# A recurrence and two MLPs in one kernel: input loads from GpSimd's queue, raw weight bits loaded two steps ahead, six result buffers, the triangular inverse begun later, products masked by VectorE

## The chip, the core and the metric

The kernel runs on one core of a Trainium2 chip, in one launch. A core has TensorE (PE) for matrix products, VectorE (DVE), ScalarE (ACT) and GpSimd (POOL) for elementwise work, and SyncE (SP), which in this kernel only issues DMA transfers. Each engine has one program and works through it in order; semaphores tie the engines together. A queue that issues transfers is such a program too: a transfer that waits holds up all that stands behind it on the same engine. The metric is device time in microseconds of one execution.

## The reference

The inputs are six arrays of 4 batches, 8 heads, 768 steps and 40 channels, and the weights of two MLPs. The recurrence goes over the 768 steps; `x` then passes through both MLPs (3072 tokens, 320 channels, 2048 hidden).

```python
for t in range(S):
    y[:, :, t] = np.einsum('bhd,bhde->bhe', rt, state)
    Sa = np.einsum('bhde,bhe->bhd', state, at)
    state_decay = state * wt[:, :, None, :] - np.einsum('bhd,bhe->bhde', Sa, bt)
    state = state_decay + np.einsum('bhd,bhe->bhde', vt, kt)
...
h = x @ w_in;  g = np.maximum(h, 0.0) ** 2;              x = g @ w_out
h = x @ w_in;  g = h * np.clip(h + 3.0, 0.0, 6.0) / 6.0; x = g @ w_out
```

All weights come as 64-bit floating point numbers and are turned into 32-bit ones on the core.

## The kernel before

**The recurrence.** The 768 steps are cut into 12 chunks of 64 steps, times 4 batches: 48 units, `i` = 0 to 47, four to a chunk. A unit is brought in by `load_pre` (its decays, keys and so on, one tile `IN` of 104 x 1029 numbers; two `IN` tiles take turns) and `load_main` (tiles `VS` and `VR`). `pre_steps` makes scaled rows: running products of the decays forwards (`EE`, L550) and backwards (`RV`, L569) by VectorE, then the scaled `RK` (L562) and `KBt` (L577) by GpSimd. `f1a` multiplies `KBt` by `RK` on TensorE (L586), copies one half of the product to `TB` and every second unit stores it to DRAM (`DT<-TB`, L592). `f1b` copies the other half to `RK` by ScalarE (L600) and multiplies it by a triangular mask on GpSimd (L601).

**The inverse.** Once the four units of a chunk have been through `f1`, `inv_gen` inverts the triangular matrices of the chunk by substitution. It loads them back from DRAM (`ML<-DT`, four loads, L622), does 31 rounds of two VectorE instructions (L632, L635), stores the result (`DIT`, `DI`) and loads it back in two shapes (`TB<-DIT` L645, `AI<-DI` L647). `merge_p` (L656) and `merge_x` (L667) put two half-size inverses together before unit 4c of the chunk is solved. `inv_gen` is a generator that runs ahead of the units: `begin` runs its loads as soon as the chunk is complete, then waits for three slots and six more ticks, and from there each `tick` adds one VectorE instruction. `need_inv` makes sure that it is done in time.

**The order of the work.** Each turn of the main loop issues the stages of neighbouring units in the order of `ORDER` (`ORDER0` before the first MLP has input): `rhs`, `umm`, `f1`, `kt`, `gmm`, `st`, `vumm`, `ys`, `mp`, `mx`, and four slots `M`. A slot takes one piece of the first MLP (or a few idle products, L817), then gives five ticks to the inverse and runs one step of the weights' conversion. `pre` runs `pre_steps` for a unit some nine ahead, with a tick after each of five steps, and then `load_pre` for the unit after next. In `ys` VectorE makes `SY` (L722), the output `XT` (L724) and the new state `STK` (L727), which `st` (L741) transposes.

**The MLPs.** A group is 512 tokens; each MLP has 6 groups. A piece is either `project_in` (8 matmuls, L222 to L226, then the activation by ScalarE and VectorE) or `out1`/`out2` (8 matmuls, L249 to L253, or 12, L261 to L263) for one of 16 slices of the hidden layer. The products are done with weights and activations each split into a high and a low part. `store1`/`store2` copy a finished group from PSUM and store it; `store2` copies four tiles `os` (L837) into a pool of three buffers and stores each (L840).

**The conversion.** `convert` turns 32 tiles of 64-bit weights to 32-bit: load of the raw `bits` (L83), then shifts and masks by VectorE (L97, L99), ScalarE (L96, L104) and GpSimd (L105), a product by VectorE (L109), a rounded copy (L122) and the rest (L154). One call of the generator is one step, in which six stages of six neighbouring tiles are issued, the load first. For the first MLP it runs from the slots, early in the recurrence, and stores the low parts (L139). For the second it runs beside the last pieces of the first, one step after every piece (`self.steps = 1`); it also stores every converted tile to DRAM (`W<-res`, L117), for `general_path`, a branch for inputs with extreme decays, whose instructions do not appear in the trace.

## Time and profile before

| what | value |
|---|---|
| median of 3 runs | 1394.53 us (1392.88 to 1398.54) |
| the profiled execution's own time | 1400.85 us |
| its span, first to last instruction | 1399.1 us |
| busy: PE, DVE, ACT, POOL | 1182.9, 841.3, 609.9, 390.7 us |
| mean granted TensorE clock | 0.899 |

Times in the trace are counted from the first instruction. A group of instructions is named by its line, engine and tiles, written out<-in. "Idle before" is the idle time of the engine just ahead of an instruction, and the name behind the arrow is what ended it. SPq is SyncE's queue of transfers.

### The profile page before, as it was taken

To read this page: it belongs to the slowest core of one execution; us is meant where nothing else is said; L and a number is where in the kernel's file an instruction comes from. 1 tells how busy PE (TensorE), PEld (TensorE's weight loads), DVE (VectorE), ACT (ScalarE), POOL (GpSimd) and SP (SyncE) were. 2 spreads that over 40 slices of the span, in tenths; PEclk is the share of its full clock that TensorE was granted. 3 is DMA by queue.
4 is the path that set the end of the run, shared out by engine and by line. 5 is a ranking of instruction groups with operands and counts; after the bars stand their busy time and mean duration, and the time that the engine had idled before them with its cause. 6 is when DMAs were issued, how large, how long until landed. Compare 5 with 4: busy or idle time off the path is not lost.

```text
span 1399.1 us, 25891 instructions
## 1 busy us (share of the span) xinstructions
PE 1182.9 (85%) x9682; PEld 1008.2 (72%) x9682; DVE 841.3 (60%) x1857; ACT 609.9 (44%) x1456; POOL 390.7 (28%) x564
## 2 busy tenths in 40 slices
PE   3178677798989999998989999876898989898895
PEld 3167567687777777777777788655697979797884
DVE  7847796767494948576765642599843434344332
ACT  4245554444544445454544443466533434333331
POOL 5685535333424433333433000255300000000000
PEclk9657767799999999999999999988999999999998
DMA  5546656565657465655654552587601010010000
GB/s 126 102 103 184 136 149 156 145 143 118 131 140 146 113 154 142 141 117 141 143 124 98 123 129 75 168 264 228 183 1 49 1 49 24 26 31 19 7 13 22
DMA packets 257221, 152.73 MB, mean 109 GB/s; under 512 B 201792, under 2 KB 220864, under 8 KB 257088
## 3 DMA queue, kind: packets, MB, share of 16 engines
q1 hardware_dynamic: 243264, 113.24, 34.2%
q10 hardware_dynamic: 13824, 37.75, 9.0%
q8 instruction: 79, 1.29, 0.4%
q14 instruction: 54, 0.44, 0.1%
HBM read 115.30 MB, written 35.65 MB: 108 GB/s over the span
## 4 chain that ended last, share of the span: by engine, by line
PE 48%; DMA 19%; DVE 17%; SPq 4%; issue 4%; ACT 4%; POOL 3%; DVEq 0%; ACTq 0%; POOLq 0%
PE h L222 9%; DMA DT<-TB 5%; PE h L224 4%; PE o L261 4%; PE o L262 4%; PE o L263 4%; DVE INV L635 3%; DVE TMP L632 3%; DMA out_dram<-os 3%; DMA W<-res 2%; PE h L225 2%; PE h L226 2%; SPq L622 2%; PE o L249 2%; PE a L586 2%
## 5 line engine op out<-in xcount | busy, mean ns | idle before, releaser
L240 DVE TENSOR_TENSOR gs<-g,gs 128x512 fp32r<-128x512 f32 x192 | 149.9, 781 | 77.8 <-ACT gs L234 65.9
L632 DVE TENSOR_TENSOR TMP<-ML,INV 128x126 f32<-128x126 f32 (+22 forms) x341 | 107.5, 315 | 77.2 <-DMA ML<-DT 69.6
L601 POOL TENSOR_TENSOR RK<-RK,mask 64x256 f32<-64x256 f32 x96 | 78.3, 816 | 254.0 <-ACT RK L600 238.1
L232 DVE SCALAR_TENSOR_TENSOR g<-r,h 128x512 f32<-128x512 f32 x96 | 66.0, 687 | 133.9 <-ACT r L231 133.9
L261 PE MATMUL o<-w_out,gs 128*128 128x320 f32 x384 | 121.0, 315 | 22.1 <-DVE os L837 20.6
L105 POOL TENSOR_TENSOR bits<-res,bits 128x384 int32<-128x384 int32 (+1 forms) x64 | 70.3, 1100 | 223.6 <-DMA wl<-LI 124.5
L231 ACT ACTIVATE r<-h,cst 128x512 f32<-128x512 f32 x96 | 66.2, 689 | 137.5 <-PE h L226 135.8
L262 PE MATMUL o<-w_lout,gs 128*128 128x320 f32 x384 | 120.1, 313 | 0.0
L263 PE MATMUL o<-w_out,gs 128*128 128x320 f32 x384 | 120.0, 312 | 0.0
L237 DVE TENSOR_TENSOR g<-r 128x512 f32<-128x512 f32 x96 | 66.5, 692 | 81.5 <-ACT r L236 81.5
L635 DVE TENSOR_TENSOR INV<-INV,TMP 128x126 f32<-128x126 f32 (+22 forms) x341 | 109.8, 322 | 8.3
L234 ACT CAST gs<-g 128x512 fp32r<-128x512 f32 x96 | 59.5, 620 | 97.4 <-DVE g L232 97.4
L222 PE MATMUL h<-xm,wl 128*128 128x512 f32 x192 | 78.5, 409 | 25.4 <-DMA wl<-LI 25.4
L261 PEld LDWEIGHTS o<-w_out,gs 128*128 128x128 f32 x384 | 73.7, 192 | 28.0 <-DVE os L837 21.9
L249 PE MATMUL o<-gs,wo_hi 128*128 128x512 f32 x192 | 90.6, 472 | 2.5 <-DVE os L827 1.7
L236 ACT ACTIVATE r<-h 128x512 f32<-128x512 f32 x96 | 57.0, 593 | 68.5 <-PE h L226 64.7
L562 POOL TENSOR_TENSOR RK<-IN,EE 40x256 f32<-40x256 f32 x82 | 66.4, 810 | 69.2 <-DVE EE L550 66.1
L687 ACT ACTIVATE VR<-a 40x256 f32<-40x256 f32 x96 | 36.3, 378 | 112.7 <-PE a L685 112.1
L222 PE MATMUL h<-xm,wi_hi 128*128 128x512 f32 x192 | 83.8, 437 | 1.9 <-ACT xm L208 1.9
L250 PE MATMUL o<-gs,wo_hi 128*128 128x512 f32 x192 | 82.7, 431 | 2.0 <-DVE gs L240 2.0
L251 PE MATMUL o<-gs,wl 128*128 128x512 f32 x192 | 81.9, 427 | 0.7 <-DMA wl<-LO 0.7
L577 POOL TENSOR_TENSOR KBt<-IN,RV 104x256 f32<-104x256 f32 x78 | 72.4, 948 | 32.5 <-DVE TMP L632 11.8
(159 smaller groups left out, 2953.1 us busy)
## 6 DMA issues: line engine op xcount, KB each, us to landing
wl<-LI ACTq DMA_DIRECT2D x48, 384.0 KB
wl<-LO ACTq DMA_DIRECT2D x48, 384.0 KB
IN<-in_pre_dram SPq DMA_DIRECT2D x44, 418.0 KB
bits<-in_moe_w_in_dram SPq DMA_DIRECT2D x32, 384.0 KB
bits<-in_moe_w_out_dram SPq DMA_DIRECT2D x32, 320.0 KB
VR<-in_vr_dram SPq DMA_DIRECT2D x96, 80.0 KB
DT<-TB SPq DMA_DIRECT2D x24, 256.0 KB
xr<-X SPq DMA_DIRECT2D x12, 512.0 KB
```

The lines of the kernel that those rows point to most:

```text
L222: nc.tensor.matmul(h, w[p][:, k], xm[:, k], start=(k + p == 0), stop=False)
L240: nc.vector.tensor_tensor(out=gs[:, 1], in0=g, in1=gs[:, 0].bitcast(FP32), op=ALU.subtract)
L249: nc.tensor.matmul(acc[d], hi, gs[:, 0], start=a, stop=False)
L250: nc.tensor.matmul(acc[d], hi, gs[:, 1], start=False, stop=False)
L251: nc.tensor.matmul(acc[d], lo, gs[:, 0], start=False, stop=z)
L261: nc.tensor.matmul(acc[q], gs[:, 0, s], hi, start=a, stop=False)
L262: nc.tensor.matmul(acc[q], gs[:, 0, s], lo, start=False, stop=False)
L263: nc.tensor.matmul(acc[q], gs[:, 1, s], hi, start=False, stop=z)
L577: e.tensor_tensor(out=kb_of(i)[:, :, 64 * x:64 * x + 64], in0=kb[:, :, x, :], in1=rr, op=ALU.mult)
L601: nc.gpsimd.tensor_tensor(out=o, in0=o, in1=mask[P].unsqueeze(1).to_broadcast([64, NP, 64]), op=ALU.mult)
L632: eng.tensor_tensor(out=tmp, in0=ml[:, s, s + 1:32].unsqueeze(2).to_broadcast([128, n, w]), in1=inv[:, s, 0:w].unsqueeze(1).to_broadcast([ ...
L635: eng.tensor_tensor(out=inv[:, s + 1:32, 0:w], in0=inv[:, s + 1:32, 0:w], in1=tmp, op=ALU.subtract)
```

## The change

It makes these edits:

- `load_pre` issues the load of `IN` from GpSimd's queue instead of SyncE's, from unit 11 on.
- `convert` issues the load of raw bits for two steps ahead, at the end of a step, instead of for one ahead at its start. Tile counts and buffers are the same.
- `f1b` multiplies the product by the mask in one VectorE instruction for each half, straight from PSUM; ScalarE's copy and GpSimd's product are gone.
- `begin` waits for five slots and no further ticks. In `ys` `STK` is made ahead of `XT`, and the three ticks come after all three.
- `piece` runs the second conversion after two of three pieces.
- `store2` takes two of its four tiles from the pool `m_o2` (two buffers) and two from the tags `wi` and `wo` of the pool `m_rot` (two buffers each), which the first MLP used for low weights.
- The stores `W<-res` are gone; `general_path` converts the raw bits itself where it needs them.

```diff
         def fourth(k):
             f, part = order[k]
             v, hi = res[k].bitcast(FP32), high_of(k)
-            if w["second"]:
-                nc.sync.dma_start(out=w["full"][f][:, 384 * part:384 * part + n_of[part]], in_=v)
-            else:
+            if not w["second"]:
                 rest[k] = scratch("rest", k).bitcast(F32R)
...
         n = len(order)
         load(0)
+        load(1)
         yield
         for r in range(n + 5):
-            if r + 1 < n:
-                load(r + 1)
             for lag, stage in ((5, sixth), (4, fifth), (3, fourth), (2, third), (1, second), (0, first)):
                 if 0 <= r - lag < n:
                     stage(r - lag)
+            if r + 2 < n:
+                load(r + 2)
             yield
...
-        for _ in range(self.steps):
+        if self.steps and (self.n_in + self.n_out) % 3:
             next(self.aside, None)
...
-        nc.sync.dma_start(out=in_of(i), in_=pre_in[c, b])
+        (nc.gpsimd if i > lag + 2 else nc.sync).dma_start(out=in_of(i), in_=pre_in[c, b])
...
         for h in range(2):
             P = slice(64 - 64 * h, 128 - 64 * h)
-            o = rk[P, :, 64 * h:64 * h + 64]
-            nc.scalar.copy(out=o, in_=ps[P, :, 64 * h:64 * h + 64])
-            nc.gpsimd.tensor_tensor(out=o, in0=o, in1=mask[P].unsqueeze(1).to_broadcast([64, NP, 64]), op=ALU.mult)
+            s = slice(64 * h, 64 * h + 64)
+            nc.vector.tensor_tensor(out=rk[P, :, s], in0=ps[P, :, s],
+                                    in1=mask[P].unsqueeze(1).to_broadcast([64, NP, 64]), op=ALU.mult)
...
             nc.vector.tensor_tensor(out=sy, in0=ps[:, :, 64:104], in1=stk, op=ALU.add)
-            tick()
+            nc.vector.tensor_tensor(out=stk, in0=sy, in1=E[:, :, 64:65].to_broadcast([104, NP, 40]), op=ALU.mult)
         nc.vector.tensor_tensor(out=x[:, :, b % 2, :], in0=ps[:, :, 0:64], in1=E[:, :, 0:64], op=ALU.mult)
-        tick()
-        if i + NB < NS:
-            nc.vector.tensor_tensor(out=stk, in0=sy, in1=E[:, :, 64:65].to_broadcast([104, NP, 40]), op=ALU.mult)
-            tick()
+        tick(3)
...
-    skip = [0]
-
     def begin():
-        skip[0] = 6 if moe.plan else 0
         next(gens[0][0])
-        gens[0][1] = 3 if moe.plan else 0
+        gens[0][1] = 5 if moe.plan else 0
...
             if not gens or gens[0][1]:
-                return
-            if skip[0]:
-                skip[0] -= 1
                 return
...
             for q in range(4):
-                o = opool.tile([128, DM], FP32, name="os")
+                o = (opool if q < 2 else moe.rot).tile([128, DM], FP32, tag=("os", "os", "wi", "wo")[q], name="os")
...
-        opool = hctx.enter_context(tc.tile_pool(name="m_o2", bufs=3))
+        opool = hctx.enter_context(tc.tile_pool(name="m_o2", bufs=2))
```

TensorE's program is the same instructions in the same order before and after. On the other engines the order moves, at three places above all.

SyncE's queue early in the recurrence, while the first MLP's weights are converted, around the last store of chunk 2's rows (`DT`): before.

```order
L592 DMA DT_164<-TB_131 2x64x512
L83 DMA bits<-in_moe_w_out_dram 128x640
L139 DMA LI_201<-rest 128x384
L532 DMA IN_98<-in_pre_dram 104x1029
L622 DMA ML<-DT_164 32x32x32 x4
L83 DMA bits<-in_moe_w_out_dram 128x640
L139 DMA LI_201<-rest 128x384
```

The same place of the same queue in the changed program.

```order
L605 DMA DT_164<-TB_131 2x64x512
L137 DMA LI_201<-rest 128x384
L83 DMA bits<-in_moe_w_out_dram 128x640
L635 DMA ML<-DT_164 32x32x32 x4
L137 DMA LI_201<-rest 128x384
L83 DMA bits<-in_moe_w_in_dram 128x768
```

The load of `IN` no longer stands ahead of the inverse's loads and the bits; it stands on GpSimd right behind the product `KBt` that frees the tile. The bits that follow are those of one tile later.

VectorE at the start of the inverse of chunk 4, once the first MLP runs in the slots: before.

```order
L696 TENSOR_TENSOR GV_138<-a,mask 128x8x64
L237 TENSOR_TENSOR g<-r 128x512
L240 TENSOR_TENSOR gs<-g,gs 128x512
L632 TENSOR_TENSOR TMP<-ML,INV 128x31
L635 TENSOR_TENSOR INV<-INV,TMP 128x31
L632 TENSOR_TENSOR TMP<-ML,INV 128x30
L635 TENSOR_TENSOR INV<-INV,TMP 128x30
L722 TENSOR_TENSOR SY_147<-a,STK_146 104x160
```

The same stretch of VectorE's program in the changed kernel, up to the first instruction of the inverse.

```order
L735 TENSOR_TENSOR SY_147<-a,STK_146 104x160
L736 TENSOR_TENSOR STK_146<-SY_147,EE_120 104x160
L737 TENSOR_TENSOR XT_148<-a,EE_120 104x4x64
L613 TENSOR_TENSOR RK_100<-a,mask 64x4x64 x2
L563 SCALAR_TENSOR_TENSOR EE_120<-IN_99,d_97 104x260
L567 TENSOR_SCALAR EC_163<-EE_120 104x4
L577 RECIPROCAL EC_163<-EC_163 104x4
L579 SCALAR_TENSOR_TENSOR DR_152<-flags,EC_163 104x4
L582 SCALAR_TENSOR_TENSOR RV_151<-IN_99,DR_152 104x260
L236 TENSOR_TENSOR g<-r 128x512
L239 TENSOR_TENSOR gs<-g,gs 128x512
L645 TENSOR_TENSOR TMP<-ML,INV 128x31
```

The first wait for `ML` now stands behind `ys` of the next unit, the two masked products, that unit's row scaling and one more piece. All later instructions of the inverse, its stores and its loads back move by one slot too (by two in chunk 3).

VectorE in the conversion of the second MLP's weights, between two activations of the first MLP (`g`, `gs`): before.

```order
L237 TENSOR_TENSOR g<-r 128x512
L240 TENSOR_TENSOR gs<-g,gs 128x512
L109 SCALAR_TENSOR_TENSOR res<-bits 128x320
L97 TENSOR_SCALAR res<-bits 128x384
L99 SCALAR_TENSOR_TENSOR res<-bits,res 128x384
L154 TENSOR_TENSOR w_lout<-res,w_out 128x320
L109 SCALAR_TENSOR_TENSOR res<-bits 128x384
L97 TENSOR_SCALAR res<-bits 128x320
L99 SCALAR_TENSOR_TENSOR res<-bits,res 128x320
L237 TENSOR_TENSOR g<-r 128x512
```

The same part of VectorE's program in the changed kernel.

```order
L236 TENSOR_TENSOR g<-r 128x512
L239 TENSOR_TENSOR gs<-g,gs 128x512
L109 SCALAR_TENSOR_TENSOR res<-bits 128x320
L97 TENSOR_SCALAR res<-bits 128x384
L99 SCALAR_TENSOR_TENSOR res<-bits,res 128x384
L236 TENSOR_TENSOR g<-r 128x512
```

Between two activations stand now one or two steps of the conversion, before always two. The whole conversion lies beside 26 pairs of `g` and `gs` in the changed program, the last 9 of them of the second MLP, against 18 before, of which one.

## Rows read from the trace of the kernel before

**Rows 1.** Busy time of each engine in four stretches (us, instructions), clock, DMA.
```profile
90.00:262.00 172.00, 125.98 (x1226) 113.24 (x1226) 128.92 (x286) 84.30 (x243) 86.29 (x111) 0.70 0.62 155
278.00:805.00 527.00, 484.99 (x5005) 399.46 (x5006) 356.75 (x934) 252.85 (x681) 183.99 (x278) 0.95 0.58 132
895.00:1005.00 110.00, 80.81 (x284) 61.79 (x285) 101.95 (x154) 67.32 (x138) 57.79 (x48) 0.84 0.69 219
1015.00:1065.00 50.00, 50.00 (x280) 45.29 (x280) 21.42 (x33) 19.91 (x31) 0.00 (x0) 1.00 0.08 22
```

**Rows 2.** Waits of TensorE, 1010 to 1400 us: total, times, longest.
```profile
PE o L261 <- DVE os L837: 20.6, 5, 4.2
```

**Rows 3.** The chain that ended last, second MLP: start us, us, what.
```profile
1066.34 5.92 DMA out_dram<-os
...
1322.90 5.79 DMA out_dram<-os
...
1381.02 5.83 DMA out_dram<-os
```

**Rows 4.** Timeline of TensorE at the first group's end, idle time in brackets.
```profile
1072.92 0.63 PE L261 MATMUL o<-w_out,gs 128*128 128x320 f32 x1 [4.19 <-DVE os L837]
```

**Rows 5.** Lines on VectorE by shape, 895 to 1000 us: busy, mean ns, idle before.
```profile
L97 DVE TENSOR_SCALAR res<-bits 128x384 uint32<-128x384 uint32 x16 | 8.7, 543 | 1.8 <-DMA W<-res 1.0 <-POOL bits L105 0.8
```

**Rows 6.** Waits of VectorE, 278 to 805 us.
```profile
DVE TMP L632 <- DMA ML<-DT: 68.1, 8, 9.8
```

**Rows 7.** Waits of TensorE, 278 to 805 us.
```profile
PE a L741 <- DVE TMP L632: 25.1, 8, 4.3
```

**Rows 8.** The chain that ended last, transfers of two inverses.
```profile
305.01 9.73 DMA DT<-TB
...
316.32 4.06 DMA ML<-DT
...
820.81 2.14 DMA AI<-DI
```

**Rows 9.** Timeline of SyncE's queue, second load of AI for chunk 4.
```profile
361.24 0.48 SPq L647 DMA_DIRECT2D AI<-DI  x1
```

**Rows 10.** Timeline of TensorE, first merge of chunks 4 and 11.
```profile
369.09 0.59 PE L656 MATMUL a<-AI,TB 32*64 32x32 f32 x14
...
822.46 0.30 PE L656 MATMUL a<-AI,TB 32*64 32x32 f32 x2
```

**Rows 11.** Lines on VectorE by shape, 278 to 805 us.
```profile
L724 DVE TENSOR_TENSOR XT<-a,EE 104x256 f32<-104x256 f32 x32 | 13.3, 416 | 0.0
```

**Rows 12.** Timeline of GpSimd within an inverse: start us, us, group.
```profile
401.37 1.52 POOL L601 TENSOR_TENSOR RK<-RK,mask 64x256 f32<-64x256 f32 x2 [8.18 <-ACT RK L600]
```

**Rows 13.** Timeline of VectorE at the same time.
```profile
401.09 0.29 DVE L632 TENSOR_TENSOR TMP<-ML,INV 128x126 f32<-128x126 f32 x1
401.42 0.84 DVE L635 TENSOR_TENSOR INV<-INV,TMP 128x126 f32<-128x126 f32 x1
402.29 0.76 DVE L632 TENSOR_TENSOR TMP<-ML,INV 128x136 f32<-128x136 f32 x1
```

**Rows 14.** Waits of VectorE, 90 to 262 us.
```profile
DVE res L97 <- DMA bits<-in_moe_w_out_dram: 35.3, 9, 6.9
```

**Rows 15.** Waits of SyncE's queue, 90 to 262 us.
```profile
SPq L532 <- DVE RV L569: 24.3, 5, 8.7
SPq L532 <- POOL KBt L577: 20.6, 7, 12.3
```

**Rows 16.** The chain that ended last, the first loads of IN.
```profile
1.70 6.06 DMA IN<-in_pre_dram
...
18.50 8.57 DMA in_e<-in_pre_dram
```

**Rows 17.** Timelines: issue of a load of IN (SyncE), its first reader (VectorE).
```profile
280.36 0.35 SPq L532 DMA_DIRECT2D IN<-in_pre_dram  x1
...
299.39 0.70 DVE L550 TENSOR_TENSOR_SCAN EE<-IN,d 104x260 f32<-104x260 f32 x1
```

21 lines of the change are left out of this document (17 added, 4 removed).

## The prediction

> **What bounds the kernel now.** I looked first at the busy time by stage, since the limits differ. In the second MLP (1015 to 1065 us) TensorE is busy all the time at full clock; in 278 to 805 us it is busy 485.0 of 527; in the two conversion stages VectorE is the fuller engine, 128.9 of 172 early and 102.0 of 110 late [rows 1]. So I asked in each stage what interrupts the engine that sets its pace, with the views of waits, and then took the price from the timeline or the chain.
>
> At the end of each group of the second MLP TensorE waits for VectorE's copy of a result, 4.19 us the first time and 20.6 in five [rows 2, 4], and that copy waits for a store of `os` to land, 5.8 to 5.9 us [rows 3]: four tiles go into three buffers. In the recurrence VectorE stands idle for 68.1 us in eight waits for `ML` [rows 6]; `SY` and `STK` are queued behind the waiting instruction, `st` waits for them, and TensorE loses 25.1 us there [rows 7]. Early, VectorE waits 35.3 us for raw bits [rows 14], while SyncE's queue stands 24.3 + 20.6 us at the load of `IN` [rows 15], with the bits behind it.
>
> **The change part by part.**
>
> *Result buffers.* From the first wait to the fifth, four groups take 1322.90 - 1066.34 = 256.6 us, 64.1 each [rows 3]. Undisturbed, 280 matmuls take 50.00 us [rows 1]; a slice has 8 + 12 matmuls, a group 16 slices, so 320 matmuls or 57.1 us. A boundary costs 7.0 us: the 4.2 of waiting and a restart at the low clock. With four free buffers the copies wait for nothing, TensorE has the next `project_in` to do meanwhile, and five boundaries give 35. At the end the fourth copy no longer waits 5.83 us for the first store [rows 3]; less an estimated 1.4 for its own time and the three stores issued ahead of its own, 4.4. Sum 39.4; if a boundary keeps a microsecond, 34.
>
> *Second conversion.* Here VectorE is busy 93% and TensorE 73% [rows 1], so the stores `W<-res` cost little: the wait for them on VectorE is 1.0 us [rows 5]. What helps is the pace. Before, 110 us carry 18 pairs of activations beside the conversion, and the 8 pairs that follow run at TensorE's pace, 8 x 3.57 = 28.6; together 138.6. After, all 26 pairs lie beside it: VectorE has 102.0 us of work and eight slices of the second MLP more, at 21.42 / 14 = 1.53 each [rows 1]: 114.2, at the same 93% 123.2. Gain 15.4. With VectorE full it would be 24.4. If the longer overlap with GpSimd stretches more of VectorE's work, I put the floor at 8.
>
> *Later inverse.* The eight stalls cost 25.1 us [rows 7] plus the slow clock behind them: a mean granted clock of 0.95 over 527 us [rows 1] is 53 us at the lower of two levels (1.2 instead of 2.4 GHz), of which some 25 are the idle time itself; the other 28 would take half as long, 14. So 39 stand to be gained, 4.9 for each inverse. The store of the rows takes 9.73 us to land and the loads 4.06 after the last issue [rows 8], from 305.0 to 320.4; VectorE got there 9.8 earlier, the longest of the waits [rows 6]. In the new order it has `ys`, the two masked products, `EE`, `RV` and another piece first: an estimated 8 us, a slot of 4.1 (527 us hold 32 units [rows 11] of four slots) and a projection with its activation. It arrives near 319; the wait left over is 1 to 2 us and behind it stands `GV`, which TensorE does not need at once. What comes late next is the end of the inverse. In chunk 4 the second load of `AI` is issued at 361.24 and lands about 2.1 later [rows 8, 9]; the first merge is at 369.09 [rows 10]. That margin of 5.7 covers the 4.9 that TensorE gains on it. Read likewise, the eight margins lie between 4.7 and 9.5 except the last, 822.46 - (820.81 + 2.14), which is spent already [rows 8, 10]. So some 5 to 6 us come back as waits at the merge, 3 of them in the last chunk. That leaves 33.
>
> *Masked products.* The nearest row for a VectorE product of PSUM and SBUF is `XT`: 104 x 256 numbers in 0.416 us [rows 11]; 256 columns is the mask's form too. Two for each of 48 units are 40 us more for VectorE (bounds 0.29, a product of half the columns [rows 13], and 0.76, GpSimd's time for the same product [rows 12]). ScalarE loses 96 copies, GpSimd 96 products. Outside the inverse and the conversions VectorE has a third of its time free and this costs nothing; within an inverse, where it is full, 2.1 turns x 0.83 = 1.8 us. But when GpSimd worked at its two products, 1.52 us, two instructions of the inverse took 0.84 and 0.76 instead of 0.29 [rows 12, 13]: 1.0 us lost in a turn, which goes away. I take 3 us off the 33 for the balance of all eight: 30. Bounds: 10, if VectorE's extra work all shows up as late merges, and 39.
>
> The Trainium skill says as much on the page "SBUF — State Buffer", section "Who interferes with whom": a VectorE instruction with two SBUF inputs contends with a GpSimd instruction that reads SBUF, one with at most one SBUF input does not. By that rule the masks cost VectorE only their own 0.83 us a turn and free all of the stretching of at most 1.5; the trace's 1.0 agrees, and the sum would be 4 us better than mine.
>
> *Loads of `IN` and bits.* Were the bits never late in the first conversion, VectorE would have 35.3 us less to wait [rows 14] and 8 units x 0.83 = 6.7 more to do: 29. The stop at `IN`, 44.9 us of queue [rows 15], goes; the bits for step r+2 can leave once the tile two steps back is done with, and they get a step more to land. Other waits sit behind this one (the inverse of chunk 2 fills VectorE for two turns), so I take 24; 8 if those take its place, 36 if everything flows. GpSimd's own price for issuing a load is in no row; between the 0.35 us of SyncE [rows 17] and 1.52, GpSimd's longest step here [rows 12], thirty-seven loads are 13 to 56 us of an engine that is busy 35% of 278 to 805 and half of 90 to 262 [rows 1], and that loses 96 x 0.76 = 73 us of products. I count nothing, as it is covered; without the cover it would be about 1 us a unit.
>
> *The rest.* `STK` ahead of `XT` gives `st` 0.4 us where TensorE waits for it, which I leave inside the margin. The branch `general_path` is not run.
>
> Sum: 39.4 + 15.4 + 30 + 24 = 108.8. Against the profiled execution's own 1400.85 us that gives 1292.0; the median of the runs is 6.3 lower, and from it the forecast is 1394.5 - 108.8 = 1285.7.
>
> **The rivals.**
>
> *The merge becomes the wait.* The inverse's way from store to merge is one chain, and it starts no earlier than before. Were it 4 us longer, through the masks in a full VectorE or a later store `DT`, each of the eight merges would wait, and the recurrence would give 5 to 8 instead of 30. Against it stand the margins of 4.7 to 9.5. Time: 1286 + 23 = 1309.
>
> *The conversions stay where they are.* VectorE may be the true bound early, with bits that come in time only to queue behind other work. For it: 75% busy at mixed work, and the turns with an inverse in them. Then 8 + 8 instead of 24 + 15.4: 1309.
>
> *Loads from GpSimd come too late.* This ends on the other side. A load of `IN` takes 6.06 to 8.57 us [rows 16]; it is issued right after `KBt`, and its first reader came 19.0 us later in a tight case [rows 17]. GpSimd might be held up in issuing by VectorE, full in the inverse. Over 37 units it takes 109 / 37 = 2.9 us lost in each to eat up all gains, which a load of 22 us would do, 2.6 times the slowest shown. At 43, five times the slowest, each would be 24 late: 1286 + 37 x 24, about 2170. Against: a load as on SyncE's queue has more than twice its time.
>
> The Trainium skill has a rule for it, on the same page under "A bandwidth-pool intuition that's wrong (but worth ruling out)": a load issued by GpSimd has its descriptors written by GpSimd, which VectorE can lock out; there 0.62 us became 3.1, five times. Whether VectorE's instructions here do that, no row of before shows, since no load left from GpSimd.
>
> **How the numbers follow.** The forecast as worked out, give or take half of its bounds, 0.60, 1266 to 1303; the merge 0.17; the conversions 0.15; late loads 0.04; all bounds on the good side at once, near 1255 (1394.5 less 39.4, 24.4, 39 and 36), 0.04. The range of eight in ten reaches from 1262 to the two rivals with some of the other's loss added, 1318. Under 0.5% is what a measurement of this kernel cannot tell from no change. All cases but the late loads end far below it: faster 0.95, same 0.01, slower 0.04.
>
> **What would show it.** No wait of L261 for the copies of `os` in the changed profile, and groups of 57 to 58 us: else the buffers are wrong. VectorE's wait for `ML` under 20 us in sum and TensorE's wait at `st` near nothing; if instead L656 or L667 waits for `AI` or `TB` by more than 10 us, the first rival holds. The wait for bits under 10 us and the first MLP's first piece some 24 us sooner. The conversion late, ending beside nine slices of the second MLP, with no time of TensorE lost after it. Were loads late, `check_w` or `EE` would wait for `IN`. The forecast is wrong most likely where VectorE has more to do than I count, since three of the four terms lean on its free time.

## The result and the profile after

The changed kernel takes 1376.16 us (median of 4 runs, 1372.11 to 1378.69) against 1396.53 for the kernel before beside it: a ratio of 0.985 (0.981 to 0.989). It is faster, but by about 20 us and not by 109, and it lies outside the range. Its profiled execution spans 1375.3 us (before 1399.1), so the two profiles differ by 23.8 us.

To see where, I timed stages by the first matmul of `ys` (L728, before L715) for the 1st, 9th and 48th unit, which the timelines put at 94.2, 258.9 and 898.6 us (before 93.9, 265.4 and 881.1), and by the first matmul with `w_lout` of the slices of the second MLP. "Recurrence" is the 9th to the 48th `ys` from here on.

| stage | before | after | change | forecast |
|---|---|---|---|---|
| 1st to 9th `ys` (first conversion) | 171.5 | 164.7 | -6.8 | -24 |
| recurrence | 615.7 | 639.7 | **+24.0** | -30 |
| 48th `ys` to the 17th slice (second conversion) | 186.3 | 177.1 | -9.2 | -15.4 |
| 17th to the 96th slice | 312.7 | 280.2 | -32.5 | -35 |
| 96th slice to the end | 19.0 | 19.4 | +0.4 | -4.4 |

With +0.3 ahead of the first `ys` this is the whole -23.8. The groups of the second MLP did nearly what was forecast; the end did not. The windows answer to the stretches of [rows 1]. Early, VectorE works 139.4 us where it worked 128.9. In 1050 to 1100 us, where a group ends at 1074, TensorE is now busy all the time (45.8 of the same 50 us before, also with the end of a group in them):

```profile
90.00:262.00 172.00, 129.37 (x1304) 116.18 (x1305) 139.43 (x313) 81.31 (x229) 76.61 (x107) 0.73 0.62 162
278.00:805.00 527.00, 476.73 (x4826) 393.96 (x4826) 365.57 (x953) 231.21 (x600) 151.51 (x241) 0.94 0.53 127
1050.00:1100.00 50.00, 50.00 (x281) 45.34 (x280) 22.51 (x34) 20.80 (x34) 0.00 (x0) 1.00 0.12 35
```

In 278 to 805 us TensorE is busy 476.7 us where it was busy 485.0. The waits of TensorE in that stretch (total, times, longest) answer to [rows 7]:

```profile
PE a L669 <- DMA AI<-DI: 25.6, 16, 3.4
PE a L698 <- ACT RHS L690: 20.8, 4, 5.5
```

VectorE's wait for `ML`, 68.1 us in [rows 6], is down to one of 1.6, as forecast, and TensorE no longer waits at `st`. In their place stand two waits that were not there: for `AI` at the merge, and for `RHS`. The first is in the timelines of SyncE's queue and of TensorE around one merge (start, duration, idle time in brackets):

```profile
428.64 0.62 SPq L653 DMA_DIRECT2D DI<-INV  x1
431.91 0.32 SPq L658 DMA_DIRECT2D TB<-DIT  x1
433.34 0.48 SPq L660 DMA_DIRECT2D AI<-DI  x1
433.86 1.02 SPq L658 DMA_DIRECT2D TB<-DIT  x2
438.12 0.57 SPq L605 DMA_DIRECT2D DT<-TB  x1
```
```profile
427.64 1.16 PE L599 MATMUL a<-RK,KBt 104*128 104x128 f32 x8
434.56 0.27 PE L669 MATMUL a<-AI,TB 32*64 32x32 f32 x2 [2.64 <-DMA AI<-DI]
435.65 0.62 PE L669 MATMUL a<-AI,TB 32*64 32x32 f32 x14 [0.82 <-DMA AI<-DI]
```

The inverse ends, its results are stored, `TB` and `AI` are loaded, and TensorE is there 3.5 us too early. The next chunk's rows are done at 428.80, but their store `DT` leaves at 438.12, 9.3 us later, since it stands on SyncE's queue behind those loads and four of `VS` and `VR`. In the kernel before it stood behind the same loads, but they left earlier. The lines of its queue one chunk sooner (`AI` is issued at 361.24 there [rows 9], and the rows are done at 366.05):

```profile
361.76 2.19 SPq L645 DMA_DIRECT2D TB<-DIT  x2
368.95 0.57 SPq L592 DMA_DIRECT2D DT<-TB  x1
378.75 3.79 SPq L622 DMA_DIRECT2D ML<-DT  x4
384.97 0.78 SPq L539 DMA_DIRECT2D VR<-in_vr_dram  x1
387.29 0.69 SPq L733 DMA_DIRECT2D X<-XT  x2
```

Over the chunks from 278 to 805 us, such a `DT`, the second of its chunk, left 0.8 to 5.1 us after its rows before and 7.1 to 10.4 us in the changed kernel.

The second wait begins on that queue as well. Its timeline in the changed kernel, ScalarE's and TensorE's, some 45 us ahead of the merge above:

```profile
373.80 2.86 SPq L635 DMA_DIRECT2D ML<-DT  x4
379.89 0.87 SPq L743 DMA_DIRECT2D X<-XT  x2
384.11 0.41 SPq L188 DMA_DIRECT2D xr<-X  x1
```
```profile
390.52 1.14 ACT L207 CAST xm<-xr 128x512 fp32r<-128x512 f32 x2 [6.66 <-DMA xr<-X]
394.85 0.28 ACT L690 COPY RHS<-a 128x160 f32<-128x160 f32 x1
```
```profile
395.19 1.08 PE L698 MATMUL a<-TB,RHS 64*40 64x64 f32 x16 [5.29 <-ACT RHS L690]
```

`ML`'s loads wait at the head of SyncE's queue until `DT` has landed. Before, VectorE stood still at the same time, and `XT` was done at 387.26, when the queue had just become free (the last `VR` at 384.97, `X<-XT` at 387.29). Now VectorE goes on and has `XT` at 376.55; its store stands behind `ML`, `VS` and `VR` until 379.89, the reload `xr` of the group of tokens comes as much later, ScalarE waits 6.66 us for it, and `RHS` is queued behind that wait. The waits of SyncE's queue in 278 to 805 us, one of the kernel before and then two of the changed one, show who holds it:

```profile
SPq L622 <- DMA DT<-TB: 44.2, 8, 9.0
```
```profile
SPq L635 <- DMA DT<-TB: 66.1, 8, 8.6
...
SPq L743 <- DVE TMP L645: 43.3, 8, 10.2
```

`ML` holds the queue for 66.1 us instead of 44.2.

One group of tokens is two chunks, so the `RHS` wait comes in every second chunk. From one `ys` to the next the changed kernel takes, over four chunks (us):

```
21.4 14.4 21.9 15.5   19.8 14.4 14.4 14.8   20.9 14.4 21.8 15.2   20.6 14.4 14.4 14.8
```

An undisturbed turn is 14.4. The chunks come out at 73.2, 63.4, 72.3 and 64.2 us.

### The profile page after: what moved, and what is told of

The parts are those of the page before. It is cut to its first block, busy times and chain, and to the rows that moved or that the text cites. A ratio compares the mean times of both kernels' runs of the same rounds, so it can differ in the third digit from the quotient of the medians.

```text
span 1375.3 us, 25761 instructions
## 1 busy us (share of the span) xinstructions
PE 1175.3 (85%) x9682; PEld 1003.9 (73%) x9682; DVE 872.8 (63%) x1953; ACT 584.9 (43%) x1360; POOL 334.3 (24%) x505
## 5 line engine op out<-in xcount | busy, mean ns | idle before, releaser
L575 POOL TENSOR_TENSOR RK<-IN,EE 40x256 f32<-40x256 f32 x82 | 60.0, 732 | 349.6 <-DVE EE L563 346.5
L645 DVE TENSOR_TENSOR TMP<-ML,INV 128x126 f32<-128x126 f32 (+22 forms) x341 | 105.3, 309 | 10.1 <-DMA ML<-DT 1.6
L648 DVE TENSOR_TENSOR INV<-INV,TMP 128x126 f32<-128x126 f32 (+22 forms) x341 | 99.4, 292 | 9.0
L669 PE MATMUL a<-AI,TB 32*64 32x32 f32 x768 | 37.8, 233 | 61.1 <-DMA AI<-DI 60.3
L248 PE MATMUL o<-gs,wo_hi 128*128 128x512 f32 x192 | 87.7, 457 | 1.2 <-DVE os L831 1.2
L590 POOL TENSOR_TENSOR KBt<-IN,RV 104x256 f32<-104x256 f32 x78 | 78.0, 1019 | 34.7 <-DVE RV L582 22.9
L260 PEld LDWEIGHTS o<-w_out,gs 128*128 128x128 f32 x384 | 72.7, 189 | 13.8 <-ACT os L831 6.2
L669 PEld LDWEIGHTS a<-AI,TB 32*64 32x64 f32 x768 | 31.6, 147 | 68.8 <-issue 53.6
```

The source lines that it names most:

```text
L248: nc.tensor.matmul(acc[d], hi, gs[:, 0], start=a, stop=False)
L260: nc.tensor.matmul(acc[q], gs[:, 0, s], hi, start=a, stop=False)
L590: e.tensor_tensor(out=kb_of(i)[:, :, 64 * x:64 * x + 64], in0=kb[:, :, x, :], in1=rr, op=ALU.mult)
L645: eng.tensor_tensor(out=tmp, in0=ml[:, s, s + 1:32].unsqueeze(2).to_broadcast([128, n, w]), in1=inv[:, s, 0:w].unsqueeze(1).to_broadcast([ ...
L648: eng.tensor_tensor(out=inv[:, s + 1:32, 0:w], in0=inv[:, s + 1:32, 0:w], in1=tmp, op=ALU.subtract)
L669: nc.tensor.matmul(ps[64 * h:64 * h + 64, p, :], tb[P, p, :], ai[P, p, :], start=True, stop=True)
```

## The experiments

Stage times of all runs, from their profiles, and the runs' ratios to the kernel before on the same chip. Code that an edit doesn't touch gives the scatter: with the changed kernel's recurrence five profiles (after, e7, e8, e15, e18) give 638.2 to 642.0 us.

| run | median | ratio to before | early | recurrence | to 17th slice |
|---|---|---|---|---|---|
| e1_start3 | 1362.5 | 0.976 (0.971-0.982) | 162.4 | 625.9 | 177.1 |
| e3_dt_ml_pool | 1426.0 | 1.020 (1.014-1.027) | 166.9 | 666.6 | 178.4 |
| e4_masks | 1381.8 | 0.988 (0.982-0.994) | 165.6 | 641.2 | 180.0 |
| e7_bits1 | 1376.9 | 0.985 (0.980-0.990) | 171.5 | 642.0 | 171.6 |
| e8_pace_buf | 1418.3 | 1.016 (1.014-1.018) | 163.6 | 640.0 | 188.5 |
| e10_ml_pool | 1381.7 | 0.989 (0.987-0.992) | 164.4 | 627.5 | 177.7 |
| e11_x_pool | 1368.4 | 0.981 (0.979-0.983) | 168.2 | 624.5 | 179.1 |
| e12_start3_in_sp | 1361.3 | 0.976 (0.973-0.978) | 164.9 | 619.6 | 177.2 |
| e13_start4 | 1354.7 | 0.967 (0.962-0.971) | 164.6 | 622.2 | 177.0 |
| e14_dt_in | 1349.6 | 0.965 (0.961-0.969) | 163.5 | 612.5 | 176.6 |
| e15_rest | 1378.0 | 0.985 (0.981-0.989) | 168.0 | 638.3 | 178.7 |
| e16_start4_x | 1363.8 | 0.975 (0.971-0.978) | 164.0 | 626.7 | 179.7 |
| e17_stale | 1356.4 | 0.967 (0.963-0.970) | 167.2 | 615.1 | 178.0 |
| e18_low_pool | 1380.7 | 0.984 (0.981-0.987) | 166.5 | 638.2 | 177.7 |
| e19_dt_pool | 1352.4 | 0.963 (0.960-0.967) | 164.4 | 617.6 | 177.7 |
| e20_bits2 | 1342.1 | 0.956 (0.952-0.959) | 164.3 | 613.5 | 168.7 |
| e21_ml_half | 1343.3 | 0.961 (0.958-0.964) | 159.2 | 608.0 | 178.2 |
| e22_vs | 1340.4 | 0.959 (0.956-0.961) | 160.5 | 610.8 | 171.5 |

The 17th to the 96th slice takes 280.2 us in all of them but e8, which has 312.8. Stage times come from one execution each: that of e12 was the fastest of its four (3.9 us below the median), that of e13 the slowest (4.7 us above it). The run of e10 is no shorter than the changed kernel's, since it loses 19 us ahead of the first `ys`.

### Is it the start of the inverse?

```diff
     def begin():
+        skip[0] = 6 if moe.plan else 0
         next(gens[0][0])
-        gens[0][1] = 5 if moe.plan else 0
+        gens[0][1] = 3 if moe.plan else 0
...
             if not gens or gens[0][1]:
+                return
+            if skip[0]:
+                skip[0] -= 1
                 return
```


> The changed kernel with one part undone: the inverse begins three pieces behind its rows' store again and lets six ticks pass. In the changed kernel the recurrence from the 9th to the 48th `ys` takes 639.7 us (before 615.7), TensorE waits 30.9 us for `AI` at L669 and 20.8 us for `RHS` at L698. Theory 1 (the inverse is one chain of store, loads, 62 steps, store, loads, and starting it two slots later ends it one slot later, at the merge): the wait for `AI` falls under 8 us, VectorE's wait for `ML` returns to 45 to 75 us, `X<-XT` no longer stands behind `ML`'s load for long, so the wait for `RHS` falls too; recurrence 606 to 624 us, run about 1352 us. Rival (the masked products fill VectorE and lengthen the inverse, wherever it starts): the recurrence stays above 630 us and the run above 1365 us.

TensorE's and VectorE's waits of e1, 260 to 900 us:
```profile
PE a L751 <- DVE STK L736: 36.7, 8, 5.8
...
DVE TMP L645 <- DMA ML<-DT: 83.5, 8, 11.8
```
Both new waits are gone, the old one is back, and larger than in [rows 6, 7]. The recurrence falls by 13.8 us, to 625.9: 1.9 above the range of theory 1 and 10.2 above the kernel before. With the masked products still in it, it is well below 639.7, so they are not what kept it there. They alone, put back:

```diff
-            nc.vector.tensor_tensor(out=rk[P, :, s], in0=ps[P, :, s],
-                                    in1=mask[P]...
+            nc.scalar.copy(out=o, in_=ps[P, :, 64 * h:64 * h + 64])
+            nc.gpsimd.tensor_tensor(out=o, in0=o, in1=mask[P]...
```


> The changed kernel with the masked products as before (ScalarE copies, GpSimd multiplies). Theory 1 (the place of the inverse sets the recurrence, not VectorE's load): recurrence from the 9th to the 48th `ys` within 6 us of the changed kernel's 639.7, early stage (first to 9th `ys`, 164.7 us) within 4 us, run 1370 to 1382 us. Rival 1 (40 us more work on a full VectorE is what lengthens the inverse): recurrence 15 us or more shorter, run under 1362 us. Rival 2 (the masks on VectorE took stretching away that GpSimd causes): recurrence 8 us or more longer, run over 1384 us.

The recurrence takes 641.2 us, the early stage 165.6 and the run 1381.8: nothing beyond the scatter. The start of the inverse explains the longer recurrence, the masks don't. Then the start between the two, alone and with `X<-XT` past the queue:

```diff
-        gens[0][1] = 5 if moe.plan else 0
+        gens[0][1] = 4 if moe.plan else 0
```


> The changed kernel with the inverse begun four pieces behind its rows' store, not five (and no ticks let pass). With five the recurrence took 639.7 us (TensorE waited 30.9 us for `AI`, 20.8 us for `RHS`), with the old start 625.9 us (TensorE waited 43 us at the transposes of `STK`, VectorE 83.5 us for `ML`). Theory 1 (from `DT` to `AI` the chain of an inverse takes 59 to 62 us and the next `DT` leaves 3 us behind `AI`, so four turns cannot fall much below 63 us, whichever engine shows the wait): the waits are shared, `AI` 8 to 25 us and the transposes of `STK` 3 to 25 us, and the recurrence lies between 612 and 630 us; run 1350 to 1366 us. Rival (there is slack in the chain and only the two ends of the range were badly placed): both waits under 8 us and the recurrence under 605 us, run under 1342 us.

> The changed kernel with the inverse begun four pieces behind and the stores `X<-XT` issued by GpSimd. With five pieces and `X<-XT` on GpSimd the recurrence took 624.5 us and the run 1368.4 us, the wait for `AI` 29.9 us. Theory 1 (chain of 63 us for four turns, the split's stall apart from it): wait for `AI` 8 to 25 us, for `RHS` under 9 us, recurrence 608 to 624 us, run 1347 to 1364 us. Rival (slack in the chain): recurrence under 603 us, run under 1341 us.

The recurrence is 622.2 and 626.7 us. I had the sharing wrong: one piece sooner already moves the whole wait from `AI` (0.9 us left) back to `STK` (32.0 + 6.9). But the rival's slack isn't there either: with none of the three starts does the profiled recurrence come under 620 us, and no run of e13 is below 1348. By the ratios four pieces are the best of the three starts, 0.967 (e1 0.976, the changed kernel 0.985).

### Which queue makes the second wait?

```diff
-            nc.sync.dma_start(out=DT[c % 2]...
+            nc.gpsimd.dma_start(out=DT[c % 2]...
-                nc.sync.dma_start(out=ml[64 * q + ...
+                nc.gpsimd.dma_start(out=ml[64 * q + ...
```


> The changed kernel with the stores `DT` and the loads `ML` issued by GpSimd instead of SyncE; the inverse still begins five pieces behind. In the changed kernel `DT` leaves 9 to 10 us after the last product of the rows (behind the loads of `TB`, `AI`, `VS`, `VR`), and `ML`'s load holds SyncE's queue 66 us in eight waits, with `X<-XT` behind it. Theory 1 (SyncE's queue is what the second stall of each group of tokens comes from: `X<-XT` late, `xr` late, ScalarE's split late, `RHS` behind it): TensorE's wait for `RHS` at L698 falls from 20.8 to under 10 us; the wait for `AI` stays near 30 us, since the steps still start with their slot; recurrence about 625 us, run about 1362 us. Rival (that stall comes from the loads of `xr` themselves, 5 to 6 us each, not from the queue): the wait for `RHS` stays above 16 us and the run within 5 us of 1376.

The `RHS` wait is gone, as theory 1 had it, and the run is 50 us slower, which neither had. SyncE's queue and TensorE at one merge of e3, where GpSimd issued `DT` at 457.38:
```profile
460.63 0.69 SPq L660 DMA_DIRECT2D AI<-DI  x1
461.36 5.75 SPq L658 DMA_DIRECT2D TB<-DIT  x2
```
```profile
468.38 0.39 PE L669 MATMUL a<-AI,TB 32*64 32x32 f32 x2 [9.49 <-DMA AI<-DI]
```
With `DT` beside them the last two loads of `TB` take 2.6 to 5.75 us to issue at the eight merges from 300 to 850 us (1.02 in the changed kernel, but up to 4.8 in the kernel before, with no `DT` beside them). What counts is when the merge can start: 14.6 to 16.4 us after the inverse's last step in seven of the eight, against 7.3 to 10.3 in the changed kernel and 7.5 to 9.4 in e10, where `ML` alone is moved. So it is the store `DT` that makes `AI` late here. On SyncE's queue it had stood behind these loads and left them alone. About 19 us of the run lie elsewhere: GpSimd computes one inverse at the start itself and now waits there for its own loads (first `ys` at 113.5 us, in e10 at 113.1). So only one of the two moved, and only the store of `XT`:

```diff
 e10: ML alone on GpSimd, DT stays
 e11: -                nc.sync.dma_start(out=dst[h], in_=x[P]...
      +                nc.gpsimd.dma_start(out=dst[h], in_=x[P]...
```


> The changed kernel with the loads `ML` alone issued by GpSimd; `DT` stays on SyncE's queue, behind the loads of `TB` and `AI`. In the changed kernel the chunks of four turns alternate between 63.4 and 72.8 us; the long ones hold the wait for `RHS` (20.8 us in four). In the run with `DT` on GpSimd too that wait was gone, but `AI` came 7 to 9 us late in each chunk, with `DT` landing beside the loads of `AI`. Theory 1 (two separate causes: `ML` at the head of SyncE's queue delays `X<-XT` and so the split; `DT` beside the loads of `AI` delays those): the wait for `RHS` falls under 8 us, the wait for `AI` stays between 22 and 36 us, the long chunks shorten to about 66 us, recurrence 605 to 622 us, run about 1350 us. Rival (one cause: the chain of an inverse is longer than four turns, and what one stall gives up the next takes): the wait for `AI` grows by what the other loses, recurrence within 8 us of 639.7, run above 1368 us.

> The changed kernel with only the stores `X<-XT` issued by GpSimd, past SyncE's queue; `ML` still holds that queue. Theory 1 (the late store is what makes the split late): `X<-XT` leaves within 1 us of the last `XT` instead of 3.3 to 5.7 us after it; the wait for `RHS` falls from 20.8 to 10 us or less, since the load of `xr` stands on SyncE's queue still, 3 to 5 us sooner; recurrence 618 to 630 us, run about 1362 us. Rival (the loads of `xr` are what is late, or GpSimd's store lands as much later as it leaves sooner): recurrence within 5 us of 639.7 and run within 5 us of 1376.

In both, `AI`'s wait stays at 29 to 30 us; `RHS`'s disappears from e10's list and is 9.1 in e11. The recurrence falls by 12.2 and 15.2 us. So there are two causes, and this is the second one's price as each cure shows it. The recurrence of e10 is 5.5 us above theory 1's range: its long chunks shorten to 67 us, about as expected, but the short ones grow to 66, and the small waits for `GV` rise from 3.0 to 7.9 us. What is left of the `RHS` wait in e11 probably comes with GpSimd's store: with the start at four pieces that wait is 0.6 us with `X<-XT` on SyncE's queue (e13) and 9.2 us with it on GpSimd's (e16), and every run of e16 is slower than any of e13.

### The loads of `IN`, and `DT` alone

```diff
 e12: e1 with
-        (nc.gpsimd if i > lag + 2 else nc.sync).dma_start(out=in_of(i), ...
+        nc.sync.dma_start(out=in_of(i), ...
 e14: e12, and e19: e1, with
-            nc.sync.dma_start(out=DT[c % 2]...
+            (nc.gpsimd if c > 1 else nc.sync).dma_start(out=DT[c % 2]...
```


> The run with the old start of the inverse (1362.5 us, recurrence 625.9 us) with the loads of `IN` back on SyncE's queue as well. With the old start the store `DT` took 10.4 to 11.5 us to land in most chunks, against 9.1 to 9.8 before the change, and VectorE waited 83.5 us for `ML` against 68.1. Theory 1 (a load of `IN` that GpSimd issues leaves while `DT` is under way and slows it, where SyncE issued it behind `DT`): `DT` lands in 9 to 10 us again, the wait for `ML` is 64 to 74 us, recurrence 612 to 620 us, and the early stage 5 to 10 us longer than 162.4; run about 1357 us. Rival (the masks or the order of `STK` and `XT` cost the 10 us): recurrence within 4 us of 625.9, wait for `ML` above 78 us.

> The run with the old start and `IN` on SyncE's queue (1361.3 us, recurrence 619.6 us) with the stores `DT` from the third chunk on issued by GpSimd. There `DT` leaves 3 to 6 us after the last product of the rows, behind the loads of `VS` and `VR`, and lands in 8.5 to 10.2 us. Theory 1 (the chain sets the pace; what is cut from it in front of `ML` is gained): `DT` leaves 1 to 1.5 us after the products, VectorE's wait for `ML` falls from 78.6 us by 8 to 30 us, the recurrence is 590 to 612 us, run 1333 to 1354 us. Rival (beside the loads of `TB` and `AI` the store lands as much later as it leaves sooner, or holds these up, as with the late start): recurrence 616 us or more, run 1357 us or more.

> The run with the old start of the inverse (1362.5 us, recurrence 625.9 us; `IN` from GpSimd) with the stores `DT` from the third chunk on issued by GpSimd. With `IN` on SyncE's queue the same edit took 11.7 us off the run, left a wait for `ML` of 68.6 us and a new one of TensorE for `VS`, 15.6 us, whose loads stand behind `IN`. Theory 1 (with `IN` on GpSimd, `VS` has nothing to stand behind, and `DT` leaves ahead of `IN`): wait for `VS` under 4 us, recurrence 600 to 610 us, run 1337 to 1349 us. Rival (`IN` beside `DT` lengthens its landing, as it did by 1.5 us before): wait for `ML` above 75 us, recurrence 612 us or more, run 1350 us or more.

e12: in its profile `ML`'s loads leave 8.5 to 10.3 us after `DT`'s issue, in e1's 9.5 to 11.6, as theory 1 had it, and the recurrence is 6.3 us shorter. But the wait for `ML` fell only to 78.6, the medians are 1.1 us apart, and the profile is of e12's fastest run: not decided. If the 6.3 us are taken as they stand, all but 3.9 of the 24 us are undone, by the start (13.8) and the place of `IN`. No run undoes the order of `STK` and `XT` alone. e14 takes 7.1 us more off the recurrence (612.5, just outside theory 1's range), and shows a new wait in the place of `STK`'s. In e19 the wait for `VS` stays without `IN` on the queue, so `IN` isn't what `VS` waits behind; the rival's reason fails too, since the wait for `ML` is 55.2 us and not above 75. TensorE's largest waits in 260 to 900 us of e14, then of e19:
```profile
PE a L688 <- DMA VS<-in_v_dram: 15.6, 7, 3.3
PE a L680 <- DMA TB<-DIT: 7.0, 2, 3.8
```
```profile
PE a L688 <- DMA VS<-in_v_dram: 18.9, 6, 6.8
PE a L669 <- DMA AI<-DI: 9.6, 4, 8.2
```

### What sets the recurrence?

```diff
 e17: e12 with
-        dt_, tb, ai = DT[c % 2], ...
+        dt_, tb, ai = DT[(c + 1) % 2 if c > 1 else c % 2], ...
 e21: e12 with
-        for q in range(2):
+        for q in range(1 if c > 1 else 2):
             ... (loads of ML)
```


> The run with the old start and `IN` on SyncE's queue (1361.3 us, recurrence 619.6 us, VectorE's wait for `ML` 78.6 us), where from the third chunk on the inverse reads `ML` from the rows of the chunk before, which landed a chunk ago: part of the computation is changed, the store of `DT` and all work of every engine stay. It takes 9 to 11 us of waiting for that store out of each inverse and nothing from VectorE. Theory 1 (the time from the rows' products to the merge, 64 us of transfers and steps, against 60.6 us of TensorE's work between them, sets the recurrence): with some 55 us it fits; the waits for `ML` fall under 30 us, TensorE's waits at `STK` and `AI` to under 12 us together, and the recurrence is 570 to 596 us, run 1312 to 1340 us. Rival (a full VectorE sets it: 40 us of masks and 62 steps at its share): recurrence 606 us or more, run 1347 us or more.

615.1 us. The number is the rival's, its reason isn't: VectorE still waits 74.8 us for `ML`, so it isn't full. SyncE's queue and VectorE's first step of one inverse in e12, then in e17:
```profile
431.82 0.56 SPq L605 DMA_DIRECT2D DT<-TB  x1
440.29 2.71 SPq L635 DMA_DIRECT2D ML<-DT  x4
446.57 0.19 DVE L645 TENSOR_TENSOR TMP<-ML,INV 128x31 f32<-128x31 f32 x1 [9.18 <-DMA ML<-DT]
```
```profile
433.30 0.56 SPq L605 DMA_DIRECT2D DT<-TB  x1
434.77 10.06 SPq L635 DMA_DIRECT2D ML<-DT  x4
448.18 0.19 DVE L645 TENSOR_TENSOR TMP<-ML,INV 128x31 f32<-128x31 f32 x1 [10.50 <-DMA ML<-DT]
```
Freed of the semaphore, the loads leave 1.5 us behind `DT`, but their issue drags on for 10.06 us, and the inverse begins 14.9 us after `DT`'s issue; with the wait it was 14.8. Over the eight inverses it is 14.2 to 15.4 without the wait and 14.7 to 15.9 with it. So it isn't the wait that keeps `ML`. That `DT` ahead of it in the same queue does is the likely reading; no run takes it apart from the other transfers of that moment.

> The run with the old start and `IN` on SyncE's queue (1361.3 us, recurrence 619.6 us, VectorE's wait for `ML` 78.6 us), where from the third chunk on only the first of `ML`'s two equal halves is loaded: the second is left out, so part of the computation is changed; two of four loads, half of the packets, all waits on semaphores and the work of all engines stay. In the run without the wait for `DT`, `ML`'s loads left at once but took 9.5 us to issue and landed no sooner. Theory 1 (what lies between the rows and the inverse is the time that the DMA engines need for the small packets of `TB`, `VR`, `DT` and `ML`, one after the other): with half of `ML`'s packets VectorE waits 15 to 32 us less for `ML`, and the recurrence is 588 to 608 us. Rival (the loads come late for another reason, a full VectorE or the time that one load takes at least): the wait for `ML` within 10 us of 78.6, recurrence 612 us or more.

Against e12 the wait for `ML` falls by 14.6 us and the recurrence by 11.6, both at the edge of theory 1: `ML`'s own packets are a part of its lateness, 1.8 us in each inverse, and not the larger one.

### The conversions and the result buffers

```diff
 e8:  os from three buffers of opool; a step of the second conversion beside each piece
 e7:  -            if r + 2 < n:
      -                load(r + 2)          (and load(r + 1) ahead of the step)
 e15: -                nc.sync.dma_start(out=w["lo" if part else "li"]...
      +                nc.scalar.dma_start(out=w["lo" if part else "li"]...
 e18: -                self.low(rest[k], v, hi, nc.vector)     (and the larger of part 1)
      +                self.low(rest[k], v, hi, nc.gpsimd)
```


> The changed kernel with the two late parts undone: three result buffers, and a step of the second conversion beside each piece. The recurrence must stay at 640 us within 4. From the 17th to the 96th slice of the second MLP the changed kernel takes 280.2 us (before 312.7); from the 48th `ys` to the 17th slice 177.1 us (before 186.3). Theory 1 (buffers and pace act in these stretches and nowhere else): 312 to 314 us and 183 to 190 us; run about 1418 us. Rival for the buffers (the gain hangs on other things in the late order): under 300 us. Rival for the pace (the 9 us come from the bits or from elsewhere, not from the pace): within 3 us of 177.1.

> The changed kernel with the bits of the conversions loaded one step ahead again, ahead of the step's work; the loads of `IN` stay with GpSimd. In the changed kernel the first eight turns take 164.7 us (before 171.5) and VectorE waits 7.8 us for bits there (before 36.2). Theory 1 (the waits for bits were cover, not cause: VectorE has other work queued on the chain of the turn, so the gain early came from the queue that `IN` no longer stops): early stage within 3 us of 164.7, run within 5 us of 1376. Rival (bits two steps ahead gave the 6.8 us): early stage 170 us or more, run 1381 us or more.

e8 gives theory 1 in all: the buffers are worth 32.6 us and the pace 11.4 (188.5 to 177.1). e7 has two opposite effects: one step ahead costs 6.8 us early and gives 5.5 back late, so its run is that of the changed kernel.

> The changed kernel with the first conversion's stores of `rest` issued by ScalarE, not SyncE. In the changed kernel's first eight turns (164.7 us) the loads of bits stand at the head of SyncE's queue for 55 us until VectorE has done with their tile (before 16.6), the stores of `rest` stand behind them, and VectorE waits 10.1 us for a store of `rest` to land, which it did not before. Theory 1 (part of the wait for bits turned into this one): that wait falls under 2 us and the eight turns take 154 to 160 us; run 1366 to 1372 us. Rival (VectorE only gets to its next wait sooner, or TensorE's own chain sets the turn): the eight turns within 4 us of 164.7, run within 5 us of 1376.

> The changed kernel with the first conversion's large differences (`rest`, L153) computed by GpSimd instead of VectorE: some 15 us less work for VectorE in the first eight turns (164.7 us, of which VectorE works 138 and waits 26), about 25 us more for GpSimd. Theory 1 (early VectorE's work and its waits in a row fill the turn, so a wait removed lets the next begin, and only less work shortens it): the eight turns take 150 to 158 us. Rival (the turn is set by the round trips of a conversion step, VectorE to GpSimd and back, or by TensorE's own chain): within 5 us of 164.7, or longer since GpSimd's part stands in each round trip.

VectorE's waits in 90 to 262 us, which answer to [rows 14], in the changed kernel and then in e15:
```profile
DVE rest L153 <- DMA LI<-rest: 10.1, 3, 4.2
...
DVE res L97 <- DMA bits<-in_moe_w_out_dram: 4.0, 1, 4.0
DVE res L97 <- DMA bits<-in_moe_w_in_dram: 3.8, 3, 1.8
```
```profile
DVE res L97 <- DMA bits<-in_moe_w_in_dram: 7.9, 2, 4.3
...
DVE res L97 <- DMA bits<-in_moe_w_out_dram: 7.8, 2, 5.9
```
Two steps ahead cut the waits for bits from 36.2 to 7.8 us, but the loads now stand at the head of SyncE's queue until their tile is free, the stores of `rest` behind them, and VectorE waits 10.1 us for those. Past the queue that wait goes and the bits' grows by 7.9. In e18 VectorE works 7.9 us less in these 172 us, but it waits 17.7 us for GpSimd's part instead:
```profile
DVE res L97 <- POOL rest L153: 17.7, 6, 3.8
```
So e18 can't tell what less work alone would give. The turns got no shorter in either run, as the rivals had it; what does set them isn't found.

### A version that beats both

e14 with two steps ahead for the first conversion's bits and one for the second's, then `VS` on GpSimd as well:

> The run with the old start, `IN` on SyncE's queue and `DT` on GpSimd's (1349.6 us) with the second conversion's bits loaded one step ahead, as before the change, the first one's two. With one step ahead in both the early stage was 171.5 us (changed kernel 164.7) and the stretch from the 48th `ys` to the 17th slice 171.6 us (changed kernel 177.1). Theory 1 (two steps ahead help early and hurt late, where the loads go beside those of `wl` that TensorE waits for): early stage within 3 us of 163.5, the late stretch 169 to 174 us, run 1341 to 1347 us. Rival (the 5.5 us were scatter): the late stretch 175 to 179 us, run within 4 us of 1349.6.

> The fastest version so far (1342.1 us: old start, `IN` on SyncE, `DT` on GpSimd, the second conversion's bits one step ahead; recurrence 613.5 us), with the loads of `VS` from the sixth unit on issued by GpSimd. TensorE waited 16.1 us for `VS` in seven stalls and 6.7 us for `TB` there, where both stand on SyncE's queue. Theory 1 (the queue is what makes `VS` late): the wait for `VS` falls under 4 us, the recurrence is 592 to 606 us, run 1322 to 1335 us. Rival (the DMA engines are full there and serve `VS` no sooner from another queue, or `TB` and `ML` take its place): recurrence within 6 us of 613.5, run within 6 us of 1342.

e20 takes 1342.1 us, 0.956 of the kernel before, and its late stretch 168.7, as theory 1 had it. e22 removes the wait for `VS`, and waits for `STK` (12.0 us instead of 2.2) and `AI` (5.2 instead of 1.2) take its place, while the one for `TB` stays at 6.5: 1340.4 us at 0.959, no difference. That is the rival.

## Why the prediction was wrong

Of the 85 us that the profile falls short of the forecast, 54 are the recurrence's, where 30 were to be gained and 24 were lost, and 17 the first conversion's.

**Result buffers: right.** No wait for `os` is left in the second MLP's groups, and the chain shows a group, 16 slices with the end of a group among them:
```profile
1275.05 0.93 PE h L221 x4
...
1332.54 0.93 PE h L221 x4
```
57.5 us, as forecast; 32.5 for 35. The 4.4 us at the end did not come. TensorE's last wait is 0.7 instead of 5.8 us, but the four stores still take 5.91 us to issue in a row (7.05 before), and the span ends 1375.3 - (1356.79 + 5.91) = 12.6 us behind the last issue, where it was 1399.1 - (1381.02 + 7.05) = 11.0.

**Second conversion: the mechanism right, 9.2 for 15.4.** The pace gave its gain (e8); the bits two steps ahead, which the forecast counted only early, cost 5.5 to 7.9 us here (177.1 against 171.6 in e7, and 176.6 in e14 against 168.7 in e20). Without that the term is 14.7 to 17.1.

**Masked products: right.** 0.422 us each (forecast 0.416), and no cost or gain that can be seen (e4). The rule of the Trainium skill's page "SBUF — State Buffer", section "Who interferes with whom", by which the sum would have been 4 us better, can't be told from the scatter here.

**Later inverse: this step failed, and with it the forecast.** It said that the margin of 5.7 us at the merge "covers the 4.9 that TensorE gains on it". The margin was real in the kernel before, where `AI` was issued 7.9 us ahead of the merge. But the start moves every step of the inverse in the program, the last one too, and the term did not take that off the margin. Its own figures would have shown it: 5.7, less 4.9, less the slot of 4.1 by which the loads back move, is 3.3 us short, and TensorE waits 25.6 / 8 = 3.2 us at a merge. `DT`, behind the same loads, left later with them (7.1 to 10.4 us after the rows; in the kernel before 0.8 to 5.1). The first rival is what happened, a wait for `AI` at nearly every merge, priced at 5 to 8 us of gain left; it left none. On top came the second wait, which no rival had: VectorE's stall had been a cover for SyncE's, and without it `X<-XT` came late behind `ML`. The start as a whole cost 13.8 us (e1), the second wait, a part of that, 12 to 15 (e10, e11, with the first one still there); the place of `IN` may have cost 6.3 (e12), which is not shown.

A further fault lies behind it: 39 us "stand to be gained" took the stalls as removable one by one. In the twelve variants that moved these waits (all but e3) its time lay between 608 and 628 us, with 42 to 60 us of TensorE's waits in 260 to 900 us (50 before, 58 after); whichever wait was taken away, others took most of its place. That some latency ahead of `ML` is the floor is likely, but not shown.

**Loads of `IN` and bits: 6.8 for 24, below its floor of 8.** The bits came as forecast, within 10 us of waiting, and they are the whole gain (e7 is back at 171.5). In VectorE's account the rest of it is taken up by larger work (139.4 for 128.9 us, [rows 1]) and the new wait for `rest`; but without that wait (e15) the turns were no shorter, so these are not shown to be the cause. The step that failed is that what VectorE no longer waits comes off the turns: 28 us of waiting went and 6.8 us came off. The second rival, the conversions at 8 + 8, came true in size (6.8 + 9.2). It and the first one came together, of which the range held only a part. `IN` on GpSimd gave nothing early that can be told (162.4 in e1, 164.9 in e12). The late loads of the third rival did not occur: the page has 37 of them,
```profile
IN<-in_pre_dram POOLq DMA_DIRECT2D x37, 418.0 KB, 4.4
```
4.4 us to landing in the median and 6.2 at most, against the 6.1 to 8.6 of [rows 16]; GpSimd took 0.6 us to issue one. The Trainium skill's warning on the page "SBUF — State Buffer", "A bandwidth-pool intuition that's wrong (but worth ruling out)", by which VectorE can lock out such a load, does not show in this trace.

What sets the early turns, the last 3.9 us of the recurrence and its floor stay open.

## What to carry to other kernels

A stall of one engine can be the cover of another queue's: before taking it away, look for what stands behind the same transfer in each queue, and ask whether that still comes in time when the engine doesn't wait. When a chain is started later to spare a wait at its head, count its end in the program's order as well, and the next chain's first transfer behind it, and don't take the margin there from the old trace as it stands: take off what the end moves. Price a prefetch separately in each stage that uses its code: here one depth was right early and wrong late.

## What the hardware showed unexpectedly

Loads that no longer waited for a store on their own queue came no sooner: four issues of `ML` took 10.06 us right behind `DT` (2.71 after its landing), and their reader started 14.9 us after `DT`'s issue instead of 14.8. The Trainium skill, page "DMA: Bandwidth & Descriptors", section "Queues, rings and completion order", says that what one engine issues goes into the same rings and is consumed there in order; e17 fits that, with `ML` behind `DT` in either case. A store moved to GpSimd's queue did hold up SyncE's loads beside it: the merge that needs them started 14.6 to 16.4 us after the inverse's last step instead of 7.3 to 10.3 (e3; 7.5 to 9.4 with `ML` alone moved, e10).
